# A new table of the order for a fused bucketed-attention and mixture-of-attention kernel

## The chip, the core and the metric

The kernel runs on one core of one Trainium2 chip. The metric is the time of one execution on the device, in microseconds (us). The core's engines are TensorE (matrix products; its loads of weights are shown apart), VectorE, ScalarE, GpSimd and SyncE; SyncE issues nearly all DMAs. In the profile they are called PE, PEld, DVE, ACT, POOL and SP.

## What is computed

First stage, for 4 batches and 8 heads of 768 rows with 64 columns: each row of q and of k gets a bucket from the signs of six projections; a query sees only keys of its own bucket. Second stage: the result, as 4 x 768 rows of 512, goes through a mixture of four causal attention heads ("experts"), of which each row uses the best two.

```python
q_bits = einsum(q, proj) > 0 ; k_bits = einsum(k, proj) > 0
mask   = q_bucket[:, None] == k_bucket[None, :]
scores = where(mask, scale * q @ k.T, -1e9)
attn   = softmax(scores) @ v                      # x, 4 x 768 x 512
logits = x @ w_gate ; topk = the two largest of 4
for e in range(4):
    a   = softmax(causal(scale * (x @ wq[e]) @ (x @ wk[e]).T))
    ye  = a @ (x @ wv[e]) @ wo[e]
    out += weight of e in the row * ye
```

## The kernel before

A unit is one head of the first stage (`("L", b, h)`, 32 of them) or one expert of the second (`("M", b, e)`, 16). The sequence `seq` lists the 48 units; the experts of a batch are mixed into the heads of the next one. For each unit, four kinds of work follow one another, always for several units at once:

- `max_steps(u)`: products of the queries with the keys into PSUM tiles `mx` (two buffers), in chunks of up to 512 columns. VectorE takes the maximum of each chunk into `pm` (`pmw` for the first eight heads). A chunk may consist of two products, for two blocks of queries, into one tile. Where a chunk meets the diagonal of a causal expert, VectorE adds the mask and takes the maximum in one operation (`scrap<-mx,causal`), one for each of the two halves.
- `shift_steps(u)`: the row of maxima is formed by VectorE (`negh`), turned by TensorE into a tile `misc`, copied as `row` by ScalarE or VectorE, and sent by a DMA into rows of the operand `qa`. It is subtracted inside the next products.
- `s_unit(u)`: `qk(c)` makes the products again, now the other way round and with the shift in them, into tiles `st` (three buffers). For a causal expert VectorE adds `mask_t` to the diagonal blocks in `st`. ScalarE makes the exponential twice, as `p` (32 bit) and `ph` (16 bit); `lo(c)` takes their difference `pl`, on GpSimd; `av(c)` multiplies `ph` and `pl` with the halves `vh` and `vl` of V into a tile `o` (one buffer). `normalise` ends the unit.
- `background` work: `prep_wide` and `prep_pair` split q and k into halves and make the signs `Mw` or `M` of the buckets (products with `pbh` and `pbl` or `pbd` into `misc`, one VectorE operation, four DMAs); `prep_v` scales V, splits it and sums it over the rows (VectorE, `misc<-vf`); `xt_steps`, `vproj_steps` (`mvh`, `mvl`, `lg`), `gate_steps`, `proj_steps`, `out_steps` make up the second stage.

Nothing of that is issued when it is written. A `Recorder` keeps all 10,808 operations with the engines that each may run on. `schedule()` then reads a table, `ORDER`: text in base 85, compressed, four rows of one byte for each operation. The first two rows say which of the operations that are left comes next, the third which of its engines it gets, the fourth how many filler products (`o<-busy`, 128x128, without use) go ahead of it:

```python
raw = np.frombuffer(zlib.decompress(base64.b85decode(ORDER)), np.uint8).reshape(4, n).astype(int)
for take, alt, fill in zip((raw[0] + 256 * raw[1]).tolist(), raw[2].tolist(), raw[3].tolist()):
    order += [self.filler] * fill
    o = left.pop(take)
    order.append((o, o.alts[alt]))
```

`issue()` walks that list, gives each new tile the next buffer of its pool, and hands the operation to its engine. Each engine works its own list off strictly in order. The waits between engines follow from the tiles: a second product into a tile comes behind a reader of that tile that the list puts between them. Since all operations are issued from one line of a helper, line 185 stands in nearly every row, and rows are told apart by the tiles' names.

Of the kernel before, what the change touches and what calls it, by code (L numbers as in the profile page):

```python
# [210 lines left out]
WN = 1  # L211
# [9 lines left out]
    "*DY=4WKEQ$T)m#l>BSjQnF>B7ri$iR@(sAfu$i|k>vl^vyjCu!`u$OVD&?w0dsVdy6J$yyHW7~7<o&VW=;){!8ICE+K+x-p1RLQEyrDI`-uTZ2<!@#*4SovW*ch>xhll`T*p=!}6+C)U"
    "$!4=TUDw>Omia4DaxTV~P~_m#zQ`$YI3$^TJf6)idc>&T|F}Qoi@V+9<1TWW34}Iy9Uo46f+ralZ?);N_R>ky>(gle&=4<Za?=kJxnHx~Zeg{uSG82%)u_U($K#XTs%9DyOND9m1V0G*"
    "Z-3Y23tIn;)iasytel>Ask5{C%&ehK?bxw{eNWY^oZ2(f6FPe9t<F<JLnjWE4wg39Rcc&@7U<2NV2>-{CEXR9rz({JwCRlA-0|tMvvIg|Z>`ijG2wO}28vYq<jJAYBS(e`n{Hm}?UnMC"
    "3f<G9kSmo2VMT|BvxPMVF;sWCtWh;g!aj0JGLWRLcgu-?H#n#a{`D9g|BYCT8kXp4xDoCbfq{X6pnqX`dEtM)|Grr1QB`#s2J7kRQOj3=2Tju{TFQaf=PFlFaFo02^?LlyKB}Nmg-TDp"
    "(Z~ye%JM5CjF(EV&xx$p8`fM)6rRI;Pmi};Hhty=kq0-a54%rT+%Z>3uLq1^saWB}!%@s^{!u;BA_EK!Wi~<EQQAX+iw_LQW`BRb8-`F1Dlss7ugq2|e6F0!7mGy=Mwk`LrUz#1l3Wt2"
    "o2{Gn_9|-FaDt5kMU|K2TqGh0cF=^3q>a;wj|RiUVgsA_-+JSJMf>$a*5z^s1x+(!v6w4Y|F4ijavGQM{B=6*)-^3_Qa<X>;T|ow#x|75^7~HR0wapz4}aKmIii@|hK()1E;wbQCza16"
    ")Amx<x<oN)Wy)o7%_%a)Vzc=(1r~pDQk-y(gBho6hMb9b(%A$^XRmXEO2rG0d(WB33iWlzDKK|QQeDXMt8hkp5dMf0Y*uvs75EjLA=Pnutio3`nT%v|IIbg!-ni-U`(v?qD8H}(<Ma4o"
    "Mi$sPJnt`;0}<0VG11*U=F5{{5nr~&Xp5hY#-hWS2xOJ%>3*A{K-L0@YMb4=qZxg=XKKfZa>O*}=jYAOeQu0#udc3!rrL}oa^vG8V-Ak6@8}KELq30#)-*+}(>0g-#EIK)zr8X)f69<2"
    "XFSuG@s%k9XIA&bI%kZD8K3-T+r$}Qbh^#K=@kz(=?;m(V6!<mzu-8#c;?KR#_V0HI%f?G@UVz4x1+e({B5xFkb)5E?Q2}k><2S2X%5#XZo6%H`P8YwlP6CiqxN@3y}p1b!`O$>x4WiR"
    "R#teJ`~1$G+m{d|q1fW$Vr=0jvDM<(9$;=|a&|TzACB!<V`6Hd#qz>JJT|v5w|!zFJ~$KGh9?!@IUXB}#kR*{D>j3>FJ~`&oozERvphEP?WsL~zBIFo=I)N{+zH-Y|LM$MWwWu}yP28g"  # L230
    "<-^N1v#YyoF3vpq=%ZtgJhJrg+!x!RrF$M)<828OlUn@v$FIW?z4Algl~?xffBEH?Z@>L(@4R#S{@eE7hJ)?+m%sergHLbf-A%lZeBP&=KmMJ^pLzU&&wc5!ryWl{^&0!6;bzS6OBh!!"
    "7czp#^;Q2fM#AyDL(?CB{Eo+HO?|`_2!*t}&#HkyK>ey;(`c{vE?w6zTsU~=rAuc_20X^Nc=4kCsD1|>|4Jf}crKTV$IqWXOx%C}$v?f%CUf)=l{(h{!~>~uMe*PF#ol}zf*^MM`1wYR"
# [1203 lines left out]
```

## Time and profile before

| | |
|---|---|
| median of three runs | 618.59 us (615.69 to 618.74) |
| the profiled execution | 618.5 us |
| its span, first to last instruction | 616.7 us |
| TensorE busy | 586.7 us, 95% |
| VectorE busy | 551.2 us, 89% |
| ScalarE busy | 525.6 us, 85% |
| GpSimd busy | 476.7 us, 77% |

The busy time of an engine is the union of its records. The end of a product is modelled, and products that follow each other closely overlap, so a busy TensorE is not one at its peak. The chain that ended last is followed back from the last instruction, at each step to what released it. In the rows, "out<-in" are the tiles written and read, "x4" is a count, and what stands behind a bar or in brackets is the idle time of the engine just before, with what ended it.

### The profile page before, as it was taken

The numbers are of one execution on the slowest core, as the hardware profiler recorded it, in microseconds if no ns is written. First come the engines' busy times: TensorE is split into PE (matmuls) and PEld (weight loads), VectorE is DVE, ScalarE is ACT, GpSimd is POOL, SyncE is SP. The second block draws the span as 40 slices with busy tenths as digits, with TensorE's granted clock in tenths as the row PEclk, the third lists the DMA queues.
The fourth block names the chain that finished last, engine by engine and source line by source line (L and its number), as shares of the span: only waits on it lengthen the run. The fifth ranks groups of instructions, "written<-read, shape, count | busy, mean of one in ns | idle before, by whom it ended". The sixth has DMA issues, their size and how long they took to land.

```text
span 616.7 us, 19646 instructions
## 1 busy us (share of the span) xinstructions
PE 586.7 (95%) x7331; PEld 416.3 (68%) x7331; DVE 551.2 (89%) x1514; ACT 525.6 (85%) x1162; POOL 476.7 (77%) x536
## 2 busy tenths in 40 slices
PE   8999999989999999889999999999999999999996
PEld 4778777766776666657666666767666767767663
DVE  7999989989999999878988999999989989757975
ACT  8989989999899999876978999997798989943873
POOL 7998988998688988866866889887757879941660
PEclk9999989999999999989999999999999999999999
DMA  5775522333213323331243231432122211102122
GB/s 146 223 186 155 131 70 74 85 93 101 53 41 100 79 51 78 93 83 36 62 129 88 55 95 32 134 95 60 48 61 82 46 42 42 50 14 47 51 101 103
DMA packets 35863, 51.07 MB, mean 83 GB/s; under 512 B 7764, under 2 KB 25656, under 8 KB 35768
## 3 DMA queue, kind: packets, MB, share of 16 engines
q1 hardware_dynamic: 35608, 49.83, 30.0%
q8 instruction: 57, 0.93, 0.6%
q14 instruction: 38, 0.31, 0.2%
q10 hardware_dynamic: 160, 0.00, 0.0%
HBM read 20.98 MB, written 6.29 MB: 44 GB/s over the span
## 4 chain that ended last, share of the span: by engine, by line
PE 50%; DVE 35%; ACT 6%; issue 5%; DMA 2%; SPq 1%; POOL 0%; DVEq 0%; ACTq 0%; POOLq 0%
PE misc L185 17%; PE st L185 14%; PE o L185 11%; DVE pm L185 9%; PE mx L185 8%; DVE misc L185 5%; DVE qk L185 4%; DVE pmw L185 4%; ACT p L185 2%; DVE xt L185 2%; DVE xp L185 2%; ACT ph L185 2%; DVE scrap L185 2%; DVE st L185 1%; DVE rden L185 1%
## 5 line engine op out<-in xcount | busy, mean ns | idle before, releaser
L185 POOL TENSOR_TENSOR pl<-p,ph 128x512 f16<-128x512 f32 (+1 forms) x377 | 417.0, 1130 | 117.7 <-PE o L185 35.1
L185 ACT ACTIVATE ph<-st 128x512 f16<-128x512 f32 (+1 forms) x380 | 218.8, 603 | 20.0 <-PE st L185 8.9
L185 ACT ACTIVATE p<-st 128x512 f32<-128x512 f32 (+1 forms) x380 | 220.3, 605 | 11.5 <-PE st L185 6.3
L185 PE MATMUL st<-qk,qk 128*128 128x256 f16 (+13 forms) x928 | 223.1, 325 | 3.6 <-DVE st L185 2.2
L185 PEld LDWEIGHTS <-ph 128*128 128x128 f16 x2944 | 169.9, 98 | 45.4 <-issue 14.2
L185 DVE TENSOR_REDUCE pm<-mx 128x2 f32<-128x512 f32 (+1 forms) x248 | 162.1, 673 | 3.8 <-PE mx L185 2.7
L185 PEld LDWEIGHTS <-pl 128*128 128x128 f16 x1472 | 136.9, 97 | 18.9 <-issue 3.8
L185 PE MATMUL mx<-qk,qk 76*128 76x512 f16 (+2 forms) x464 | 135.8, 330 | 11.7 <-DVE pm L185 7.6
L185 PEld LDWEIGHTS <-qk 128*128 128x128 f16 (+4 forms) x1248 | 108.2, 98 | 54.2 <-issue 14.5
L185 PE MATMUL o<-vh,ph 128*128 128x66 f16 (+1 forms) x1136 | 141.7, 195 | 2.2 <-DVE yn L185 1.4
L185 PE MATMUL o<-vh,pl 128*128 128x66 f16 (+1 forms) x1136 | 142.1, 194 | 0.0
L185 PE MATMUL o<-vl,ph 128*128 128x64 f16 x1136 | 140.8, 193 | 0.0
L185 PE MATMUL misc<-xt,wqk_h 128*128 128x384 f16 x256 | 58.8, 326 | 0.0
L185 DVE CUSTOM_DVE_ANT_0 scrap<-mx,causal 128x512 bf16<-128x512 f32 (+2 forms) x96 | 44.4, 462 | 7.1 <-PE mx L185 5.6
L185 DVE TENSOR_REDUCE pmw<-mx 128x2 f32<-128x512 f32 x68 | 45.1, 681 | 3.7 <-PE mx L185 3.4
L185 PE MATMUL o<-mvh,ph 128*128 128x65 f16 x336 | 40.0, 194 | 1.4 <-DVE xp L185 1.1
L185 PE MATMUL o<-mvl,ph 128*128 128x64 f16 x336 | 40.0, 192 | 1.4 <-DVE yn L185 1.4
L185 PE MATMUL o<-mvh,pl 128*128 128x65 f16 x336 | 40.2, 193 | 0.0
L185 PEld LDWEIGHTS <-xt 128*128 128x128 f16 x324 | 29.8, 97 | 10.7 <-DVE mvl L185 1.1
L185 PE MATMUL misc<-wvg_h,xt 128*128 128x260 f16 x192 | 33.4, 274 | 0.4 <-DVE mvl L185 0.4
L185 DVE TENSOR_TENSOR st<-st,mask_t 128x128 f32<-128x128 f32 x96 | 27.5, 292 | 6.5 <-PE st L185 5.0
L185 PEld LDWEIGHTS <-wqk_h 128*128 128x128 f16 x256 | 23.4, 97 | 13.4 <-issue 0.9
(216 smaller groups left out, 963.1 us busy)
## 6 DMA issues: line engine op xcount, KB each, us to landing
qk<-qk SPq DMA_DIRECT2D x128, 96.0 KB
...
```

The source lines that it names most:

```text
L185: getattr(getattr(self.nc, e), m)(*[real(x) for x in args], **{k: real(x) for k, x in kw.items()})
```

## The change

The text of `ORDER` is replaced; nothing else is. Of its lines the first ones stand here:

```diff
@@ -214,77 +214,76 @@
 MEANB = 3
 
 ORDER = (
-    "c-rlpd30RYec$K3`}TSJyf@36eZ_2;1v3~72I~;}LVzG4f&}+n5=kx8Vp581OQIxeakW^oEh~~@Q?(UUQXJbl&SF<doVICC>zuafNt&Mi(KdE-($oK%o}T{U_IKY57Lu|<$r1%p^U=Z6"
...
+    "c-rlpX^<S}dEck+Yr1>-?zyMuzOS9#nZ1wMUF?BtcX2I_#V!EiAP62JVG%qeng>LXA|;WbNQzNxN)bVdkt{NyBwMys#Z(d}A6!<Yq)ME!V}D4+uEeGIgUg9h<>Yy1W-o}cND&YLa(-1k"
...
 )
```

Decoded, the two tables hold the same 10,808 operations. They differ in this:

- The order of every engine. In TensorE's queue of 7232 products 1133 keep their place.
- The engine of 101 operations that two may run: 18 fewer for VectorE (1418 to 1400), 16 more for ScalarE, two more for GpSimd.
- The number of filler products, 61 in the old table and 73 in the new one; 14 of them now stand first in TensorE's queue.
- No reader of a tile `mx` or `st` stands any longer between two products into that tile; in the old table this is so for 10 tiles `mx` and 3 tiles `st`.

The new table is said to come from a search that used the true time of VectorE's sums of V, and in which all products into a PSUM tile come ahead of its readers, and these keep one sequence.

## Rows read from the trace of the kernel before

**Rows 1.** The page: span, and busy us (share of span) xinstructions of each engine.

```profile
span 616.7 us, 19646 instructions
PE 586.7 (95%) x7331; PEld 416.3 (68%) x7331; DVE 551.2 (89%) x1514; ACT 525.6 (85%) x1162; POOL 476.7 (77%) x536
```

**Rows 2.** The page: the chain that ended last, by engine.

```profile
PE 50%; DVE 35%; ACT 6%; issue 5%; DMA 2%; SPq 1%; POOL 0%; DVEq 0%; ACTq 0%; POOLq 0%
```

**Rows 3.** TensorE's waits: who waited for whom, us in total, times, longest.

```profile
PE mx L185 <- DVE pm L185: 7.6, 15, 2.3
...
PE st L185 <- DVE st L185: 2.2, 3, 1.2
```

**Rows 4.** Timeline of TensorE: start, us, product, [idle before]; first, second, last of nine parted products.

```profile
266.20 0.27 PE L185 MATMUL mx<-qk,qk 65*128 65x256 f16 x1 [2.25 <-DVE pm L185]
...
330.30 0.27 PE L185 MATMUL st<-qk,qk 67*128 67x128 f16 x2 [1.21 <-DVE st L185]
...
580.39 0.22 PE L185 MATMUL st<-qk,qk 128*128 128x128 f16 x1 [0.70 <-DVE st L185]
```

**Rows 5.** Timeline of VectorE ahead of 266.20: a sum of V and the parted tile's first reader.

```profile
262.79 1.56 DVE L185 TENSOR_REDUCE misc<-vf 128x128 f32<-128x768 f32 x1
...
265.73 0.41 DVE L185 CUSTOM_DVE_ANT_0 scrap<-mx,causal 128x256 bf16<-128x256 f32 x1
```

**Rows 6.** Windows: length, busy us of PE, PEld, DVE, ACT, POOL, clock; one wait.

```profile
264.00:266.20 2.20, 0.00 (x0) 0.00 (x0) 2.15 (x7) 1.90 (x6) 1.75 (x3) 1.00 0.07 16
...
267.30:270.70 3.40, 3.40 (x31) 1.43 (x28) 0.85 (x2) 1.41 (x3) 1.16 (x1) 0.50 0.39 125
...
74.89 0.47 PE L185 MATMUL mx<-qk,qk 76*128 76x512 f32 x1 [1.35 <-DMA qk<-Mw]
...
76.10:82.90 6.80, 6.80 (x59) 5.36 (x56) 4.82 (x8) 4.69 (x10) 4.20 (x5) 0.50 0.58 143
```

**Rows 7.** Groups of instructions: xcount | busy us, mean ns | idle before; sums and maxima of V.

```profile
L185 DVE TENSOR_REDUCE misc<-vf 128x128 f32<-128x768 f32 x16 | 25.1, 1571 | 0.0
...
L185 DVE TENSOR_REDUCE mqk<-natv 128x1 bf16<-128x768 f32 x14 | 13.2, 943 | 0.0
```

**Rows 8.** Groups: forms that change engine most, on VectorE; one on ScalarE.

```profile
L185 DVE CAST qk<-mx 128x384 f16<-128x384 f32 x24 | 13.1, 548 | 0.2 <-ACT mx L185 0.2
...
L185 ACT ACTIVATE qk<-mx 128x384 f16<-128x384 f32 x24 | 12.5, 528 | 0.1
...
L185 DVE TENSOR_SCALAR xt<-misc,xs 128x384 f16<-128x384 f32 x15 | 9.1, 608 | 0.9 <-PE misc L185 0.9
...
L185 DVE TENSOR_SCALAR ot<-misc,xs 128x512 f32<-128x512 f32 x4 | 3.0, 750 | 1.0 <-PE misc L185 0.5 <-PE o L185 0.5
...
L185 DVE TENSOR_SCALAR lg<-misc,xs 128x4 f32<-128x4 f32 x12 | 2.6, 220 | 3.2 <-ACT mvh L185 3.0
```

**Rows 9.** Groups of TensorE: fillers, and products of signs at the start and later; its first product.

```profile
L185 PE MATMUL o<-busy 128*128 128x128 bf16 x61 | 5.6, 230 | 0.0
...
L185 PE MATMUL misc<-natk,pbd 128*32 128x384 f32 (+1 forms) x22 | 4.1, 383 | 0.0
...
L185 PE MATMUL st<-natk,pbe 128*32 128x384 f32 x4 | 2.8, 847 | 0.0
...
2.55 0.41 PE L185 MATMUL misc<-one,pat 1*32 1x1 bf16 x4 [2.55 <-POOL pat L185]
```

**Rows 10.** The chain in order of time: start, us, what.

```profile
129.92 1.11 PE o L185 x37
...
159.19 1.95 PE misc L185 x12
...
266.65 0.34 PE st L185 x3
```

**Rows 11.** Timeline of one trip of a row of maxima: first and last product.

```profile
129.23 0.25 PE L185 MATMUL misc<-identh,negh 128*72 128x128 f16 x1 [0.45 <-DVE negh L185]
...
131.99 0.60 PE L185 MATMUL st<-qk,qk 78*128 78x512 f16 x2
```

More of the change, by code (lines that the diff above doesn't have):

```diff
@@ L221 @@
[L221 to L232, printed above, removed]
@@ L285 @@
[L285 to L287 removed]
+    "c-rlpX^<S}dEck+Yr1>-?zyMuzOS9#nZ1wMUF?BtcX2I_#V!EiAP62JVG%qeng>LXA|;WbNQzNxN)bVdkt{NyBwMys#Z(d}A6!<Yq)ME!V}D4+uEeGIgUg9h<>Yy1W-o}cND&YLa(-1k"
+    "Gnnaq`#qlH|GW(Vcez$rnU4iS%i)7q|B9dERhwnpmaL1q&gyQ(#d$o8B=S7X(QO!)OQlqb>R~vFvf`|Zx{nwqNS3a-2637p9ET)KB17tgo3OnVpW9VT6fiTFi)FP;lywZlX9SIa6PSr;"
@@ new lines @@
+    "VS@?#{i^EKY?m4^727aO)(`@MrZS2mk%nm=ltoQcce>^m7yU<$2p&NYIL9)^$EQt`Hw1n6n0JQKX6-(EV#=E2Eem};#@7ahhsVdqkLh~m@ITje{a}nIjjExl$F$w9^0Ip9Q0c)3CF+v<"
+    "H*vc_+wSZJbt|)lY-X%Y&Ydd!KbV)2(EzfBTTy!Q+;VDaC{fzLFbjo!Lti`bHDhscaKR9`mov+|gtYh7xT;zU3z}*OLf$>P!TkK_o)+QEt}UoLv%W!jW=7%aV?Iezt-+Czk=<L6<(-;5"
+    "FhK248dFoHy5o&_!{M-2txio%ag|E2%=T<ycsN%mo7HLw)^c_>AQ$|K(#+@cV{qh^9KdHggH8rhmSx2$N3=6PbsVQssn}eJGlN>h6Am}^x~|(X1Q*pDC#$G#Pcj%ZVu3&!$aqXgQC=$?"
+    "_M}p1Dz(gDbI|cz6i4NR{M9&fTv=IJ33Fn&81BG^+GIlUR4T<Mx8VyZvEDMeTRB`(9LHWU4jaalu``e~QZqASJB-sl$qWXq;Bl+n+=cMZQ3PU4NL&;H5xdoFEY?$x$Myd!X{_Qyw+@A<"
@@ new lines @@
+    "|KtgDP_$ewpW6#4#`3Z;Jgk0d$h1=Z{rxZWw_)BL8=BJU^+vtfY<eb+9zDQu%gaNTE{!N*u~Hcr2=(_jT1+<2c=*0z?*_xblf&ygxMvSLFITFy(|1|bQ+>U&=hu2y1*Yd@d)Ws6cCh`S"
+    "-htWKryI?gT8+zTBhB&3R))6IJD7PP8qEli@BS&QOJIEdj`{Iod2DogI+Om1KDoNar&7s3{$ouAM&k+QZ#jAZcy?fe-ig*=$Hu^UPMqii3hiDu=$_t&<Yk!MyFE-vD3{AKl2F_Z&*VLf"
+    "oMGg8eR=uCREkS--1Ao805q5=22!P3hld?^bqhUNt~|CC!v}^xB3Es%k83n6yRQ!{wx@@$?#vM7bYIDgr<zS#PoroRq1~}46VuU*vGUfracp(G$QL9jm(y7(t=g&@AKnDk-*E~q#|de{"
+    "v=&Tm8_5oU4opq?-Ob>H+npNaXt?BOKl>Ro6fYDCfjn0V)_$t%RbymCw*q>hz<>b-vJr5mqJf+uJ-LD1M7-N%wSYD{im}7^5dKb0?(x1Q2qC`&Gr&})r@t{hT>(Fq@}-jKd0EW8D5hS>"
@@ new lines @@
+    "NUn4~pQ~*m_VjR*Xwvp=kjO9ogPZ%wP)cYvg$aHJ7#E^_Bf|W=P>Vv~6sizB`4+-=M#OJRLv`uM5iI3i;|^vrPO1YeDOM`+iOhfD;pIIj3=XE#c$Uayyn>TU8h-ztNVFK~vC=-HgcXa4"
+    "aeID#9+t|R%h^WfqN;b`*fGnBknvzJ8qG!#U{%qUW0<vT_?=9KTY@OMK~^nIPA=;<?+;~078fm_rg7d=I~$3$`8B_4d%aV>#s)q0!8!`7yXUo?9S$7|%xiNk)Y(~bX6DB;2e)9_)B6Gn"
+    "%owFlADLJ^>|L3gVx$T2B492qhSZ6R!}raM1yyx;D^ne=PHg}w@)7XBY0~zR<5N=uWIJk1PMRctr_PUE!~XqaV@qRWjnUEL8?eT_N*+FZSXl;Ci1+)|T}w+#Ju_sqIUD^qFdF#r@DB8A"
+    "bar-jZZ;NM*dV%hIeO^Oo;^ESsU$i*y(2mkotukJ&&)K_(P*r>YuET81h+Z*)zyuU7cRu^xMS?-?T!;WbM?%b9fzjxyKiqSmfLl_e<-)-$dMy^4o}SQ-gV+%%h65C+xNtKz&!r=<8R=P"
@@ new lines @@
+    "E$&>p_-%0uU;Ck7eB!s)S(Dy=`|Z`W3+dzEI)DDnH`BMLU;ih-xwQD|`7eIvMIwoxlK$qY4sUMd(gROcpSk)R{w3YEuUw3li7Qu}mmNp5A`h4s!YPYOBvMB51=D=qFr!h+aZcZ9++iBr"
+    "6Ob`@^WJ;$Pm%XL`lzBwS~jce!)IG0Qz=IM%2)W<+S*zs^B{>|`htvo`tu2?FV26e#qF`tvAcTi6c;`h9r8XtvF8j39(?azg0RbgWPIk{dylj+4*UK7g9rUR`}g0wPEWu;vG2|e{1+a6"
+    "_yT#?(eopt=gy7ty^jE|e*aa($ncMU>*x5v4=(=Rd%^$iSHFMvgLe<{_fKDX5u5tf%hNA$zw_6V^WXZG*?jhyx87>LKKts-Z~y*wzA&@)rSGrvM}PGB?|ttZzt!ZXSAO`zS6=;tKUm>;"
+    "*OB#K*S-yW<x3a=wte*Jrw_h?aJ~Ne>(5@@|A)ihc=uhfrYkQYn|cI}=iqqjt+!mRXP^4QxpTkq#vAzSXRltp`qXQ$-FF{a@ps;N2ggstsz3Tqzk`$bo&Vyc$6iD{^5w689US6$^10`("
@@ new lines @@
+    "lCQlsKmWkR`$@!QI9_UVp>^iam+=>R!AOYbYtIq&`faz}OF#Yen>2k7bSc=8sjt3TC6-SU<SPVm=+M7>@hm}HI305xI(F>Xp(uWM1;_Dyd-fbUa1#GJyu}yM3)X~}rSX~b=iz+}Yx7?*"
+    "Y-X%R!jfVHK`cRMT<}i(ugvNyQKsoRIz~@U#yhvA52D|QU{J&Jd1L0>xiSul#lUGCSEJFRF+3(ol1xZ=+ZS|4jJTzpQCtaxalgk?=Y74hx2H$OUwP#fzJb5wZo%NZgxIx9`doZ|J`UNT"
+    "#RPNd&wQ-SayE+TjbUEn@mh^25vM48yqa8mmTIxQ%(9P%*be=0K;RwFdRe=VVm9y~a9NHNqEY^5S&nwoC}#*E&V<Hwonly4f@@`#&1U(Gu*wQTE+=e2^P51Kz%cLyHKglqd4OUmp^vf<"
+    "EX{(V;Ax(U3i35{R55E)Ly1H})6!nAm!d1y|6xE|n|_+e`Ka|AL_=oX(FQckB&kfaiNQ5$bch@bS-en`3P`#54CsDIEN-fs0S!X3p5yyExXb09nBb9lvM`K1^NXQaG)+GJ^wVsDOpuo^"
@@ new lines @@
+    "FGQbsB1#gZ_cx1rIBew}%B|zL@N_t}$vC1g77ma6PdudSf2H?FAR*cQzEE2N25U7Ru?3h@!X_=Z1p>Y5W|>fk2*Pyv{HE75A#PEBL4=3o(12w<X!%=Y;TS+4WM2od_n?>b{JDotDak?$"
+    "3g^U3#+^=kQgt~QmPnxzl}W)D%7<EZ=k@Y7Kw6f@sk&lnm~E?CP4)Zr_D%dOw2R@k6cttaALvj>)2>{(f(tS)J{}CZ1-Bb&HC7jduPd#^R}|$=sMsW-WtXDhhVNE*hWGi}2B9yZSEr3?"
+    "Djt54Z_2U;c5PityOt^x#lp{_iDHILdpvHp^e3W^<1lEH(=eaUZHXddF^pSRI1vd59_c_yX3AxlQn$dd9^TeC(^S<+2PVgQGIj>6x&Stl&3c?P!>UO};TbtHI!ca!MaE(*i+W5G;c#iA"
+    "rl8;Mlr8-msCHYU7cmaK<$JiQw=8m8Z*QT#4RAe{if8Cpo=L8cimKdo*Il{67H1*NwLd+M?axptmZkJ;{DEpb9&b&{J@-&FeP@ikqYMR>?SL0JsZj@1@=r%bqRx<ih-hCuXl>Z~Ud(YK"
@@ new lines @@
+    "xg2iH;QByIqu?z$iuuxC#I{2Hch;aNSopja2G5Jxj^7{fM>YutM>>Q+{QN~v54CR~SP7N;D5~ZQ5#C(3Q$^tz2z%P&F(cK*MTm-fa%=&N%l|#@yWb_e2-&hIAJ6H$_cc6#_x7Uj17B;%"
+    "EK4O@RK6q{jIMtkf`#smYMO#d6)3uie#P{_Ie%&2>$bjD78PS1hIhm7m$4NtIV}g4-8}7Pc<5;;#O*TrIgab&z)CsJwmAh{%fzAOS5WghI0WnWY~r}xAvU-LDX;}WPy^nOq6mi1vOFxQ"
+    "GHjfax7IOL4wW4;-`N#F@->XPIm>dJjKhHC(MhJPs4gGnp(s{N`U990C~rdI1c_?%d@u-$oXav9LW{WxRFv-Z+U+fXXiMIW5hMj&YTag>gnDI|8FCNii{ya=Hq9#r5`@WWnr!bYys&Hk"
+    "u3cP94vTRR!sCz|BK&0f#EHRl1`I5o%|aeylgZB{ler`t-m)bTkGo<-?7ZW3awifKiNx4gYh$6!?c}*Oas14gGi9sMI7!+ze%!l~Z6)vo*=Bf{OS<E3eAYD+>6@OOW~QcCz6wDb$EkBD"
@@ new lines @@
+    "@-wF>t?!_<s!*B!#l}Kz;GpLK;wQK5-roVb+^GmaEbaR2It!l(Km72+6uuZe)xK8{KYG;k-Jc-FFODCL$M@~WmM+}=;Mx`%c>Muf#XpTVe*;lpxeqaaFE!V9cz;Wup_@%FEWsU5ojS$C"
+    "AI_blPVB_y&m4E1Adej*PM&-SB>39evDMFh_Tt6pD$1gQFb1LTHQ}D2yM>`4fjEEio|ABKgI^a2^a+$!=@oi$7{Wv2)Aw_9J1^gr-vPhgo}tfX#?zovGH_aZBP3B1_AUrQr2@*TToU%9"
+    "fV&VBb~ceY#ye&i9P1Z^!J*Z<FyN}9tWfk7D+doQ@r!)E$h*u<aBvpCi&I+|ThUW`2Sx*8zNn8?{h_d~s~&mOKdTwT)|6+%Eo9X!GezXh9>%f?mX#Ax`zc9A4W!c%$cM!GZjMNUjS4(Y"
+    ">05SZ2Del7g+uic)##;av<wC|LRGRbGqrjuSKWRl$e8~AOr;f4OMQKdMOST4tz4*=T)n+Stw#2c<J%!(sWed<ER|dhoQlWNrBWPnK8`1dY|CY{NVVaKL^hk)q3c1t*#W-xI?6`6mLm~j"
@@ new lines @@
+    "x{UM)BmC$`D3gLxIiHxA2nI!a1Y@#-3p&=Com!0!1Sne9?V_K`W_`Xi#X&3z+8D-oUxH8s<L8y2qA{w0qTVxUPIs-Z1WzaUIIk#-$Hj9hG>%AfpuyDtplOZ}(f<cr%?Fu4V2Sl~WPps6"
+    "2E+WvRsyUgaa{<<;{`qxilLSMa?_<KmZeO<o#F1jLCRNqBfz?p+BYPb6v>uUOeU#hPl*)8qYw!qbT$%!3`;I7><t8VbAJCKwJ_>$S?kEiM8C<h178L7p;vkb*$pcD_K{5f3Y+tITrFJ}"
+    "|BNh8q7Ok>t<icT*gv>M^=Vq>thNasT3T|2f}zm=4jl}Kq2G%$NLZN7Mx%3q(k83Oop>GH4Baj>5O4(y(hzl1Bq6dxC=f}S(aMu$W`gC%Jlu#tire{{&O1djpaq#ZigLlS>4Hxn+k3+O"
+    ">zl(J`6-xk(xMWHW_)5R(l|s^6dP$_kO8&x!}=e>cqw{(d^kq^D~9Q8&Q-3l`gy=#=`TM|_0mkO!qY0pfrtNln%__jX&0YJ3Mi{U4d!%Y!~DEJ#-R2GD~+~0us8u#3ex+L(Vs#%g~FVo"
@@ new lines @@
+    "$VTfXBnW{(BvP-N=2$K_;tP_7L2e;Re#LRb&Fwh0Vg<QBBN*T7uajX$Z;RXDx-%<gXG_Z@CTx3*f}4eFR%kF3DwjF0>h=DZtB!G5w+AdcnRRng)R6k)dTZ-Amf;G!#4>dM>5M2zGf)q{"
+    "BgSK*KSsBufj7EN0HhZLl)#ruLDS49VN&$ZM<M^h;yCJKVVAlO?Z$QN!M1ym8$p`2K<CLa;b})WNr@}UL^LYNVLarOByf^BNeYET$q<@4>Ae=n>`;986~S)FT19cTBgsJ#7jcf`O}^u;"
+    "vd(dY=n*i{z}=cgOA^iez7&#zb92n%q8iz|m-Vr%7cwjz;~1L7DJ4L!_&33+bjs_^r$D7BDTVWRNRnmSMhO|EH~0(KtY?rEwS)Bw#X+IBm*jJ#{W&sS1TDd`B+KlpR+(pk?*M7cA;{!6"
+    "zxmBrJe?+pF?w{g+1vbQk%^6c_c+}{z~mDID8770`4M55RtSE9z{cWO!S+w<vD|TrMR>_N;YxT@%cM3Qj?e_P0r7V*K!Jc37&ZhVlkurxz2#w7;J`Cnx&uymabyr=YwFvfoNDi!nc*-A"
@@ new lines @@
+    "b)FZbhGa=UR((4#Pcmr}c^WD?AtFcOM5(0I6ovAE2JB=lH!pev9LPe8c=*jX-~8*K9b}=9VKuOH4XwT;Wj8C4Nc)YsEQ!J3ql{!4s^=lMD9d&mQ7I7lUa>7AH738Ns-hx_!Ncz6lkS)("
+    "I^M-$H+Vdh@CF?1E?^jn*L<2k+G<0W+F4nWP%AL|a{RsE`KVX)SP+f<zF^R&dwJ2#LpaZ5cu7$<H%_%y-2)En5u8$q_eA)d6zs`VdmwDht|O?ZZbpSK@1}TsmQA(Px8BD>HIz)UdZ~1<"
+    "6mo0%Hir(KJ9H?|x^u+R(hhzBLpqdBA_Xe4k;rVMx`Y0c=}KjCU~;ko1y?WR3$);zg&valrSkkH+`)r&&^sXh#&K#r$2Joa8+)G^%OsN!kLF@zbO~S<EA4$vX0kmInL@cRHhFG<gs?h("
+    "=N4v>QPM+Xq`7ZksZtpNaj>$<o@3PI%dnOkGAs)RAy^cJHuccPufQ_rIdD6Wuzjab*DAv!?1omP>4BxCm-qQsR+eZ*q3QiJy|nbmR?eTNq0mX<flpITZf&hFIYZs~;A2$Ad;a|Si*TI3"
@@ new lines @@
+    "|NQyGMDP+hcp7;0w13;x<DVsC!w)q`QU|FHDRlNguV)9m?}cND#o+Rjqw}4<K&`lIb&g$K-MO}Q@-}Av*y`L7{8K3LG6(OtcoB)id-j1_pFMku=jV5xd+OZXtN8KN<BvTC(dFs-sa52F"
+    "F!%#-EbRNYG)<u!oulSA-E)O<yQyVC82EGHAj(7pxd_+d?6R-K`g}OVG<%`#0Z-Z+`28$|nZcf(ignB|j+pO(!7!v1&}q#(OxsYdtCD2A2a+BESD-;NieAO0J>lu;u*VZ@&bebT%{?_`"
+    "_?s%-50RPP8n<~G!hYT~<L!I3qRFslXfNkZrRWe8gG{v(!66Su20DRlU?9@pAF0$Uc$4Y45KB=NTml0g12-CGD@C@z=Bw<|Ql%4Y+4ZVF!xcB5?zNxf?g0&zWB6QdN3}YY$u{}k-dqZj"
+    "HN&{FbcUwWPPAN3Q1SKJKaLy>N}NazvbAl4noLBfcDALr5Yj|3w!<!K|4l0vwE|7#aw_#B^fZG-`*QI~f$=f#o<bu+5@VQAEsa5$h3M=NZL3eKN<}S~Gq7m+yvjh;_mn1k4Y>8ROAb@a"
@@ new lines @@
+    "Z0;YsJMQY@`j9&HA72pc#x6B>0}B!CMkeu(y}Iv~FTY?Ou#a?lv5(h`;varoH_MEWTa_#MK2HCjVF|nGg!20isMvK`DEuS4_#<xpgIPXyeH`ZFmjI|6HZJ@owUCeR5?}Lt2D|R##jnHc"
+    "V7JzS<Da~ca4U;&>=rPon_HHAtnHor6)qq@#N}Nx?9yH3E?t}J(xvMTU8m~OjpW_2bVI_gJT~k`wvT-zON8C@i-3Lj&SPDd=}tg*hCi;uz`C}0!^VBf|H}-lYXF~+K4YKwE_V6YEC=>0"
+    "o{imd7Ke51=#$vR_iL!wulm(Zy+QEF$Pw7B(w`e{QQgGf<<@k!uH|-lpLT$`y8BaI-@El!7yIA~fOS{#W*ahgBOAbOSbwpP(A;mCrNX+N^9k-K_VJrs?1uOIMzzt^DBVQ<>+m`3dfnpJ"
+    "?o8YNufyxLvH!kR#QVLWbnO=({9o*B{ZEC6_iAd}KVo6fi@f<~`j_AE19XY+hN&)Hx^(H%rAwDCUAlDX(xpq6E?v5G>C&Z3mo8npbm`KiOP4NPx^(H%rOPLl{|}<*9S#"
```

74 lines of the change are left out of this document (16 added, 58 removed).

## The prediction

> **What bounds the kernel now.** I read the page first. The span is 616.7 us in an execution of 618.5 us, so 1.8 us lie outside it. TensorE is busy 586.7 us, VectorE 551.2, ScalarE 525.6, GpSimd 476.7 [rows 1]. The chain that ended last is half TensorE and 35% VectorE; ScalarE has 6% [rows 2]. So the reader should see two engines that take turns at being last, and 30.0 us (616.7 - 586.7) in which TensorE does nothing. That is the most that a new order could gain on TensorE, short of what the clock gives back. No product is added to or taken from the computation.
>
> Next the waits of TensorE. The largest is a product into `mx` that waits for VectorE's `pm`: 7.6 us in 15 waits. A product into `st` that waits for VectorE's `st` costs 2.2 us in 3 [rows 3]. The timeline shows which products these are. In the old table two products that write one PSUM tile are often parted: between them stands VectorE's reader of the first half. I decoded both tables (order, engine and number of filler products of each of the 10,808 operations) and counted tiles of `mx` and `st` whose first reader stands ahead of a later product into the same tile: 13 in the old table (10 of `mx`, 3 of `st`), none in the new one. In the trace the second product starts as soon as the first reader is done: at 266.20 where the reader ends at 266.14 [rows 4, 5]. Nine of the 13 show TensorE idle, for 2.25 + 1.21 + 0.38 + 0.36 + 0.36 + 0.19 + 0.55 + 0.28 + 0.70 = 6.28 us in the order of time [rows 4]; the other four show no wait. The three in `st` are all of the 2.2 us of `st` waits; the six in `mx` are 4.1 of the 7.6 us of `mx` waits.
>
> The longest of them shows how it comes about. On VectorE the first reader stands behind a sum of V (1.56 us from 262.79) and four operations more that follow it without a gap; it starts at 265.73 [rows 5]. TensorE does nothing from 264.0 to 266.2, and from 267.3 to 270.7 its granted clock is 0.50, the lower level, while VectorE is busy 0.85 of 3.4 us. A second such place: TensorE waits 1.35 us for the DMA `qk<-Mw`, and from 76.1 to 82.9 the granted clock is again 0.50 [rows 6].
>
> **The change part by part.** Only the table changes. All 7232 products stay; in TensorE's queue half of them move by at most 3 places and nine in ten lie between 13 places earlier and 14 later. It is the old plan revised, so I cost what differs in kind.
>
> *Products kept together.* Removed: the 6.28 us of idle time, and the low clock that follows the longest wait. In those 3.4 us TensorE was busy throughout at half speed, so 1.7 us are lost. Together 8.0 us. Not all of it reaches the end: where TensorE no longer waits for this reader, the next thing due from VectorE may be late. On the chain TensorE has 50 parts to VectorE's 35, so I let 50/85 = 0.59 through: **-4.7 us**, bounds 0 (VectorE is late everywhere) and -8.0.
>
> *The true time of the sums of V.* A sum takes 1571 ns, sixteen of them 25.1 us. A maximum over the same 128x768 input takes 943 ns [rows 7]. The diff doesn't say what the old search believed; if it priced the sum like that maximum, its plan was late by 628 ns sixteen times, 10.0 us of VectorE. The new table cannot shorten a sum, only place other work over it. At VectorE's share of the chain 10.0 x 0.35 = 3.5 us; I take half, **-1.8 us**. Bounds 0 and -3.5.
>
> *Engines.* The table gives VectorE 18 operations fewer, ScalarE 16 more, GpSimd two more (two `pl` subtractions of the last unit). The net moves from VectorE to ScalarE are nine `lg`, six `qk` halves, three `xt`, two outputs and two `mean`, less three `yth`, two `row` and one of the first halves. At the rows' means (220, 548, 608, 750 ns) [rows 8] this is 9 x 0.22 + 6 x 0.55 + 3 x 0.61 + 2 x 0.75 = 8.6 us, about 8 with the small ones and the two `pl` set off. ScalarE gains about as much, say 7: a `qk` half takes it 528 ns [rows 8]. VectorE's 8 x 0.35 = 2.8 us less ScalarE's 7 x 0.06 = 0.4 us gives **-2.4 us**, bounds 0 and -8. What hides it on ScalarE is its 91 us of idle time; where ScalarE is the last, the whole 7 us would show.
>
> *Fillers.* Sixty-one filler products become 73. Fourteen now stand at the head of TensorE's queue, where the first product of any kind began at 2.55 us [rows 9], so they fill a wait for GpSimd. If all twelve more lay on the path they would cost 12 x 0.092 (61 took 5.6 us) = 1.1 us. They could also gain: the four `st` records of the signs at the start took 847 ns where the same shape took 383 on the mean of the run [rows 9]. That is 4 x 0.46 = 1.9 us, and twice that with the like ones of `mx`; the records overlap in pairs, so 1.9 us in all. I take **0**, with -1.9 to +1.1 as the bounds.
>
> *Trips through a DMA.* Here the new table is tighter. I counted the TensorE work that stands between the transposing product of a row of maxima and the first product that reads that row. A product into `o` counts 30 ns (37 took 1.11 us on the chain) and one of 384 columns 162 ns (12 took 1.95 us) [rows 10]. The tenth percentile of this cover falls from 3.2 to 2.4 us and the median from 4.1 to 3.7. Of the 46 trips 2 had less than 2.7 us in the old table, 12 have so in the new one. What a trip needs: the product starts at 129.23, and its row is read at 131.99, after a copy and a DMA, with no wait shown: 2.76 us from start to start, 2.7 from the end of the product's slot [rows 11]. The new shortfall against 2.6 to 2.8 us is 3.3 to 5.7 us over all trips, the old one 0.8 to 1.2. The work between also takes longer than its bare count because TensorE waits elsewhere, so much of this is covered. The signs `M` go the same way: twelve trips whose least cover falls from 3.7 to 3.5 us and the median from 4.6 to 4.2. Priced as the rows are, this may add 2 us of shortfall. Bounds 0 and +6.5; I take **+2.9 us**, under half. Other loads go earlier: those of `natq` and `natk` in the first batch stand at least 11.9 us of products ahead of their use instead of 6.5, which hides them anyway.
>
> Sum: -4.7 - 1.8 - 2.4 + 0 + 2.9 = -6.0 us on 618.5: **612.5 us**. The profiled execution lies 0.1 us under the median of the three runs (618.59), so no step is needed between them.
>
> **The rivals.**
> - *The waits for `mx` stay.* The pool has two buffers, so a product waits for the reader of the product two back, and VectorE's queue is hardly shorter: at 264.3 to 265.7 it worked off that queue without a pause [rows 5]. Then of part one only the `st` waits go (2.2 x 0.59 = 1.3 us), parts two and three give half (2.1), and the trips take 2.9: 618.5 - 1.3 - 2.1 + 2.9 = **618 us**. For it: VectorE has 35% of the chain. Against: 4.1 of the 7.6 us of `mx` waits belong to products that write the tile they already hold [rows 4], and the parted product held up work that needs nothing of VectorE: three products into another tile, `st`, followed within 0.8 us of the one at 266.20 [rows 10]. Chance 0.25. (The Trainium skill, Perfetto Trace Analysis, Optimization Strategy, speaks for this rival: a gap that keeps returning on the engine that should be full can mean too few buffers for the next tile. For those 4.1 us the trace disagrees, for the other 3.5 it may agree.)
> - *The trips decide; slower.* One mechanism: products that read a row or the signs come before the DMA has landed. It decides if a trip needs 3.1 us, as most of the trips with little cover took, rather than the 2.7 of the shortest. Then 17 trips fall short, by 8.6 us against 1.6, and the signs add 2. [...] With the gains as forecast: 618.5 - 8.9 + 9.0 + 3.4 = **622 us**. Chance 0.13.
> - *More is set free.* The 1.35 us wait for `Mw` and the low clock behind it go too (cover 5.6 us against 5.2) and the parted products give all they cost: 612.5 - 3.3 - 1.35 - 2 = **606 us**. Chance 0.15.
> - *The table doesn't do what it says.* The sums of V stay where they were; only the parted products go: 618.5 - 4.7 + 2.9, about **617 us**. Chance 0.07, counted within half a per cent.
>
> **How the numbers follow.** The forecast has the other 0.40. A measurement of this kernel can tell about 0.5% (3.1 us), so faster means below 615.5 and slower above 621.7. Faster: 0.40 + 0.15 and a little of the first rival, 0.57. Same: 0.28. Slower: 0.15, which is the second rival and a little for what neither table's plan foresaw. The range takes in the forecast's own bounds, the fourth rival and the first, and reaches to the third: 605 to 620. The likeliest case alone spans 608 to 616.
>
> **What would show it right or wrong.** Right: no `PE st <- DVE st` wait, `mx <- pm` waits of some 3.5 us, no low clock near 267 us, TensorE's idle time near 25 us, VectorE's busy time near 543 and ScalarE's near 533. The trips are as I say if TensorE's waits and weight loads name DMAs of `row` and `M` for under 3 us in all. Wrong: TensorE's idle time at 30 us or more with other names in its waits; a new stretch of clock 0.50; or DMA waits of 6 us and more.

## The result and the profile after

The changed kernel takes **593.11 us** (median; 591.06 to 593.92), the kernel before on the same chip 618.66: a ratio of 0.9588 with a 95% interval of 0.9554 to 0.9623, 25.5 us less. The forecast was 612.5 us and its range ended at 605. The sign was right and the size was four times too small. The profiled execution took 593.65 us. In the runs beside the experiments the kernel before took 613.6 to 614.7 us where its mean granted clock was 0.999 or more, and up to 622.8 us where it was lower, while the changed kernel showed 0.999 or more in all its runs: so some 4 of the 25.5 us are stretches at the lower clock.

The page of the changed kernel: span, busy us (share) of each engine, and the chain that ended last by engine.

```profile
span 591.9 us, 19679 instructions
...
PE 576.6 (97%) x7343; PEld 414.6 (70%) x7343; DVE 542.7 (92%) x1496; ACT 523.5 (88%) x1178; POOL 477.7 (81%) x538
...
PE 71%; ACT 14%; DVE 6%; DMA 3%; issue 2%; POOL 2%; SPq 0%; ACTq 0%; POOLq 0%; DVEq 0%
```

Beside [rows 1] the span is 24.8 us shorter. TensorE's idle time fell from 30.0 us to 15.3 (591.9 - 576.6), its busy time by 10.1. VectorE had 35% of the chain [rows 2] and now has 6%.

TensorE's waits in the changed kernel: who waited for whom, us in total, times, longest.

```profile
PE st L185 <- DMA qk<-roww: 1.7, 1, 1.7
PE st L185 <- ACT ph L185: 1.1, 3, 0.6
PE mx L185 <- DVE pm L185: 1.1, 3, 0.6
PE o L185 <- DVE busy L185: 1.1, 1, 1.1
PE mx L185 <- DMA qk<-M: 0.9, 1, 0.9
PE st L185 <- ACT p L185: 0.8, 2, 0.6
PE st L185 <- DMA qk<-row: 0.6, 2, 0.4
PE misc L185 <- DVE yn L185: 0.5, 1, 0.5
PE mx L185 <- DVE pmw L185: 0.5, 1, 0.5
```

The wait for `pm` fell from 7.6 us to 1.1, and the wait of `st` for VectorE is gone [rows 3]. Others for VectorE, which the prediction had not priced, are gone or nearly so. In the kernel before they were these, in the same view:

```profile
PE o L185 <- DVE yn L185: 2.8, 2, 1.4
...
PE o L185 <- DVE xp L185: 1.7, 4, 0.9
PE mx L185 <- DVE pmw L185: 1.5, 4, 0.5
```

All rows of that view with VectorE as the releaser add up to 18.4 us in 35 waits before and 4.2 us in 10 after. Nothing comparable took their place: waits for ScalarE went from 1.1 to 2.1 us, for DMAs from 1.9 to 3.2.

The stretch 250 to 275 us, where the longest parted product stood: length, busy us of PE, PEld, DVE, ACT, POOL, granted clock, DMA share and GB/s; first before, then after.

```profile
250.00:275.00 25.00, 21.17 (x279) 15.10 (x278) 19.98 (x56) 19.75 (x44) 17.32 (x18) 0.93 0.28 79
```

```profile
250.00:275.00 25.00, 25.00 (x302) 18.19 (x301) 24.28 (x65) 21.04 (x50) 19.78 (x19) 1.00 0.38 103
```

After, TensorE never pauses here and the clock is never 0.50; nor is it near 76 us. Both low stretches of before [rows 6] are gone. They were 6.8 and 3.4 us of busy TensorE at half speed, which is 5.1 us lost in that execution.

So the 24.8 us of the span are 14.7 us of idle time (the waits for VectorE alone fell by 14.2), 5.1 us of clock, and 5.0 us of other busy time, whose cause stays open.

### The profile page after: what moved, and what is told of

Read it like the earlier page. It is cut to its first block, busy times and chain, and to the rows that moved or that the text cites. A ratio compares the mean times of both kernels' runs of the same rounds, so it can differ in the third digit from the quotient of the medians.

```text
span 591.9 us, 19679 instructions
## 1 busy us (share of the span) xinstructions
PE 576.6 (97%) x7343; PEld 414.6 (70%) x7343; DVE 542.7 (92%) x1496; ACT 523.5 (88%) x1178; POOL 477.7 (81%) x538
## 4 chain that ended last, share of the span: by engine, by line
PE 71%; ACT 14%; DVE 6%; DMA 3%; issue 2%; POOL 2%; SPq 0%; ACTq 0%; POOLq 0%; DVEq 0%
PE misc L185 23%; PE st L185 21%; PE o L185 16%; PE mx L185 11%; ACT p L185 5%; ACT ph L185 5%; DVE pm L185 2%; DVE misc L185 1%; ACT xt L185 1%; POOL pl L185 1%; ACT mx L185 1%; DVE pmw L185 1%; DMA qk<-M 1%; DMA qk<-roww 1%; ACT qk L185 1%
## 5 line engine op out<-in xcount | busy, mean ns | idle before, releaser
L185 POOL TENSOR_TENSOR pl<-p,ph 128x512 f16<-128x512 f32 (+2 forms) x379 | 418.4, 1129 | 86.2 <-ACT ph L185 19.7
L185 ACT ACTIVATE p<-st 128x512 f32<-128x512 f32 (+1 forms) x380 | 230.3, 646 | 11.3 <-PE st L185 9.8
L185 ACT ACTIVATE ph<-st 128x512 f16<-128x512 f32 (+1 forms) x380 | 228.2, 644 | 9.2 <-DVE st L185 2.1
L185 PE MATMUL st<-qk,qk 128*128 128x512 f16 (+13 forms) x928 | 224.4, 325 | 4.5 <-DMA qk<-roww 1.7
L185 PE MATMUL o<-vh,pl 128*128 128x66 f16 (+1 forms) x1136 | 139.3, 193 | 0.1
L185 PEld LDWEIGHTS <-qk 128*128 128x128 f16 (+4 forms) x1248 | 106.8, 98 | 46.3 <-issue 9.9
L185 PE MATMUL o<-vl,ph 128*128 128x64 f16 x1136 | 138.6, 192 | 0.0
L185 PE MATMUL mx<-qk,qk 76*128 76x512 f16 (+2 forms) x464 | 133.2, 326 | 2.9 <-DVE pm L185 1.1
L185 PE MATMUL misc<-xt,wqk_h 128*128 128x384 f16 x256 | 56.9, 325 | 0.0
L185 POOL TENSOR_TENSOR vl<-vf,vh 128x384 f16<-128x384 f32 x32 | 29.7, 930 | 9.9 <-ACT vh L185 9.8
```

The lines of the kernel that those rows point to most:

```text
L185: getattr(getattr(self.nc, e), m)(*[real(x) for x in args], **{k: real(x) for k, x in kw.items()})
```

## The experiments

Each kernel is the changed kernel's program with another list in `ORDER` (or one line changed, where shown). "The old list" is that of the kernel before. Ratios are to runs of the kernel before on the same chip; the gains in experiments 1, 3 and 4 are read from them. Waits are sums over the rows of TensorE's waits in the profiled execution.

**1. The old list with the 13 parted tiles kept together** (`old_joined`). The second product goes ahead of the first reader:

```diff
 product 1 -> mx
-reader 1 of mx
 (what stood between)
-product 2 -> mx
+product 2 -> mx
+reader 1 of mx
```

> The old table, and in it the later products into the 13 parted tiles stand directly ahead of the tile's first reader; nothing else moves. If the parted products are the cause (6.3 us of waits and 1.7 us of low clock behind the longest), about 610.5 us and no low clock near 267 us. If VectorE's next reader is simply late in their place, 616 to 619 us. If most of the 25 us comes from the order as a whole, this gives no more than 8 of them.

611.73 us, ratio 0.9914 (0.9869 to 0.996): 5.3 us gained. TensorE's waits:

```profile
PE mx L185 <- DVE pm L185: 3.9, 9, 0.9
PE o L185 <- DVE yn L185: 2.7, 2, 1.4
PE misc L185 <- POOL pat L185: 2.6, 1, 2.6
PE o L185 <- DVE xp L185: 2.0, 4, 0.9
PE mx L185 <- DVE pmw L185: 1.2, 4, 0.5
```

The `mx` waits fall by 3.7 us, the `st` waits for VectorE go, and so does the low clock at 267 us (1.00 from 265 to 272 us). Runs of both kernels with a mean granted clock of 0.999 or more differ by as much on the mean: 613.95 us before, 608.7 us here. The term of -4.7 us was of the right size. The waits for `yn`, `xp` and `pmw` stay.

**2. The same 13 tiles parted in the new list** (`new_parted13`), experiment 1 backwards.

> The new table with the same 13 tiles parted again: in 10 tiles mx the second product comes behind the first reader, in 3 tiles st the first reader comes ahead of the second product. If parted products cost what their waits showed, 599 to 601 us, with TensorE waits for pm and st that are absent in the new kernel. If TensorE finds other work or the wait is hidden, 593 to 595 us.

598.63 us, 0.9717 (0.9643 to 0.9792): 5.5 us more than the changed kernel's 593.11 (7.9 by the two ratios), with `mx <- pm` at 5.1 us in 10 waits. The price is no smaller in the better plan.

**3. The old list with quick sums of V** (`old_fastsum`). The sum reads neighbouring numbers, so means of V come from other numbers; its time is that of the maximum [rows 7].

```diff
-nc.vector.tensor_reduce(total, whole.rearrange("p j c -> p c j"), axis=AX.X, op=OP.add)
+nc.vector.tensor_reduce(total, vf.rearrange("p j c -> p (j c)")[:, 0:NT * 2 * D].rearrange("p (c j) -> p c j", j=NT), axis=AX.X, op=OP.add)
```

> The old table; the sums of V are taken over neighbouring elements, so that one should last near the 943 ns of a maximum over 768 elements instead of 1571 ns. This changes what is summed: the means of V, used only for rows without a partner, are other numbers. If the old plan was wrong by the length of the sums and this is the cause of most of the gain, about 600 to 605 us. If at VectorE's share of the chain, 615 us. If the sums hardly mattered, 617 to 619 us.

608.54 us, 0.9885 (0.9802 to 0.9968): 7.1 us gained. The group of the sums (xcount | busy us, mean ns | idle before) and the first of TensorE's waits:

```profile
L185 DVE TENSOR_REDUCE misc<-vf 128x128 f32<-128x768 f32 x16 | 15.2, 951 | 0.0
```

```profile
PE mx L185 <- DVE pm L185: 5.7, 10, 2.3
...
PE st L185 <- DVE st L185: 2.2, 3, 1.2
```

Taking 9.9 us from VectorE (25.1 to 15.2) gave 7.1: 0.7 us for each, though the interval (2.0 to 12.2 us) is wide.

**4. Both in the old list** (`old_joined_fastsum`).

> The old table with the 13 tiles joined and with the shorter sums of V (other numbers for the means). Alone the two gave 5.3 and 7.1 us. If they are separate causes, 12.4 us under the kernel before: a ratio of 0.980. If they are one cause (a VectorE that is late, seen at two places), 7 to 8 us: 0.988. What is then left up to the new kernel's 0.959 is neither of them.

604.3 us, 0.9784 (0.9723 to 0.9846): 13.3 us. The two gains add up (5.3 + 7.1 = 12.4). Of the 25.5 us, half is explained by them; some 12 us are not. TensorE's waits for VectorE are still 10.8 us in 21.

**5. The new list with quick sums** (`new_fastsum`) and **with sums twice as long** (`new_longsum`, each number added twice and the mean halved). The first is the edit of experiment 3.

```diff
-nc.vector.tensor_reduce(total, whole.rearrange("p j c -> p c j"), axis=AX.X, op=OP.add)
+nc.vector.tensor_reduce(total, whole.rearrange("p j c -> p c j")[:, :, None, :].to_broadcast([128, 2 * D, 2, NT]), axis=AX.XY, op=OP.add)
```

> The new table with the same shorter sums (other numbers for the means of V). If the new plan has hidden the sums' true time, 592 to 594 us, as without it. If VectorE's time simply counts everywhere, 10 us of it less at the new chain's 6% give 0.6 us, and at the old chain's 35% 3.5 us: 589.6 us.

> The new table, each sum of V taken twice over (and the means scaled by half), so that it lasts about 1.5 us more than the plan has for it, 24 us of VectorE in all. If what hurts is time that the plan does not know of, at the rate of the old table's 7.1 us for 10, then 17 us more than the new kernel: 610 us. If VectorE's time has a price that does not depend on the plan, at the 1.8 us for 10 that shorter sums gave the new table, 4.3 us more: 597 us.

Quick sums: 591.33 us, 0.9596 (0.9523 to 0.9668), no difference from the changed kernel. Long sums: 614.38 us, 0.9954 (0.9924 to 0.9983), 21 us more. Some 3 of the 21 are a stretch at a lower clock (0.52 from 36.7 to 43.5 us of its profile; the mean clock of its ten runs is 0.985 to 0.998). In the long one:

```profile
L185 DVE TENSOR_REDUCE misc<-vf 128x128 f32<-128x1536 f32 x16 | 47.6, 2973 | 0.0
```

```profile
PE mx L185 <- DVE pm L185: 6.5, 9, 1.4
PE misc L185 <- DVE qk L185: 2.6, 3, 1.2
PE mx L185 <- DVE pmw L185: 2.6, 4, 1.0
PE mx L185 <- DVE xt L185: 1.4, 1, 1.4
```

The same operations, at the same places: 9.9 us less gain at most 1.8 us, 22.5 us more cost 21, or some 18 without the clock. The new list has room for the sum as long as it is, and not for one nearly twice as long, though VectorE idles for 49 us of the span. Where in between the room ends was not measured.

**6. Order and engines crossed** (`old_newengines`, `new_oldengines`): the old order with the new choice of engine, and the other way round. Decoded operation by operation, the two tables give 82 operations another engine; the 101 named above and in what was expected is too many, while the net moves (18, 16 and two) hold.

> The old order with the new table's choice of engine for the 101 operations that differ. If VectorE's 8 us less work count by themselves, as the prediction had it, 2.4 us faster: 0.996. If they carry the rest of the gain, 8 us and more: 0.987. If the choice only fits the order it was made with, the same time or slower.

> The new order with the old choice of engines, so VectorE has 18 operations more. If VectorE's time counts by itself, 2.4 us over the new kernel: 595.5 us. If the choice carries the rest of the gain, 600 to 603 us. If it makes no difference in this order, 593 us.

| | old engines | new engines |
|---|---|---|
| old order | 1 | 1.0195 (1.0134 to 1.0256) |
| new order | 1.0062 (1.0025 to 1.0099) | 0.9588 (0.9554 to 0.9623) |

Waits of the old order with new engines, then of the new order with old engines:

```profile
PE mx L185 <- DVE pm L185: 8.5, 15, 2.3
PE st L185 <- ACT p L185: 3.1, 6, 1.4
PE o L185 <- DVE yn L185: 2.7, 3, 1.4
```

```profile
PE st L185 <- POOL pbe L185: 2.7, 1, 2.7
PE st L185 <- ACT p L185: 2.4, 6, 0.7
PE mx L185 <- DVE pm L185: 2.4, 6, 0.6
PE o L185 <- DVE none L185: 2.3, 3, 1.7
```

Either half alone is slower than before, by 12.7 and 4.2 us; together they gain 25. The first has VectorE busy 6 us less than before (545.1) and is slower all the same. What an engine choice is worth can't be read from busy times.

**7. Only 28 short operations on their old engines** (`new_smallold`): 14 `row` copies and 14 `none`, of 150 to 275 ns each.

> The changed kernel with its own order, but the old choice of engine for 28 short operations alone (14 that write the rows, 14 that zero or copy, 150 to 275 ns each, some 6 us of busy time in all that change engine). The whole old choice cost 28 us in this order. If an operation on another engine costs by its length: 592 to 593. If it costs by where it now stands in that engine's queue, ahead of or behind work it was not placed by: 596 or more.

600.23 us, 0.9713 (0.9655 to 0.9771): some 7.5 us more than the changed kernel, while VectorE's busy time rises by 1.0 us and ScalarE's by 1.3. The largest wait is now this one:

```profile
PE o L185 <- DVE none L185: 2.3, 3, 1.7
```

`none` takes 0.2 us, and TensorE waits up to 1.7 us for it: in VectorE's queue a sum of V, a `row` and two `qk` run ahead of it without a pause, from 112.31 to 115.01 us. An operation on another engine costs by its place there, not by its length. These waits are 2.3 of the 7.5 us; the rest lies in smaller ones and was not traced one by one.

**8. Where along the list the other 12 us lie.** Four hybrids, all without parted tiles and with quick sums: one list up to a place, the other list from there, cut where `normalise` begins for unit 5 (the "norm"; some 100 us) or for unit 24 (some 325 us).

```diff
-order = old[:]
+order = new[:k] + [o for o in old if o not in new[:k]]     # and the same with old and new changed over
```

> The changed kernel's table up to the norm of the second stage (list position 1663, some 100 us), then the old table with the parted products kept together; the sums of V are the fast ones, so means of V come from other numbers. Both neighbours of this kernel are measured: the old table joined with fast sums 604.3, the new table with fast sums 591.3, so 13 us lie between. Theory A, the first 100 us carry about 5 us of it (the wait for Mw, the stretch at the low clock behind it): 599. Theory B, the gain of the order is spread over the whole list: 602. Theory C, nothing of the head counts, since the VectorE is caught up later: 604.

> The other half: the old table (joined, fast sums) up to the same norm (list position 1652), then the changed kernel's table. Theory A: 596 to 597. Theory B: 593. Theory C: 591. If both halves lose more than they should together (sum of the two losses over 13 us), the plan is worth something only as a whole.

> The changed kernel's table up to the norm of unit 24 (list position 6042, some 325 us), then the old table with the parted products kept together; fast sums, so means of V come from other numbers. Between the two whole tables with fast sums lie 604.3 and 591.3 us. TensorE's waits for VectorE after 320 us are 4.3 us in the old joined one and 0 in the new one, between 104 and 320 us 5.2 and 1.9. Theory A, the gain lies all along the list in these waits and nothing is caught up: 597 to 598, TensorE's waits for VectorE some 8 us. Theory B, what the first half gains the second half gives back: 602 to 604. Theory C, only the middle part (100 to 320 us) counts: 592 to 594.

> The other half: the old table (joined, fast sums) up to the norm of unit 24 (list position 6030), then the changed kernel's table. Theory A: 596 to 597, TensorE's waits for VectorE some 6 us. Theory B: 591 to 593. Theory C: 601 to 603.

| which part is the new list | us | ratio | TensorE's waits for VectorE |
|---|---|---|---|
| none (experiment 4) | 604.3 | 0.9784 (0.9723 to 0.9846) | 10.8 us in 21 |
| up to unit 5 | 605.9 | 0.9791 (0.9726 to 0.9855) | 12.1 in 22 |
| up to unit 24 | 598.55 | 0.9679 (0.9616 to 0.9742) | 8.0 in 17 |
| from unit 24 | 599.79 | 0.9689 (0.9625 to 0.9753) | 7.3 in 16 |
| from unit 5 | 592.41 | 0.9597 (0.9537 to 0.9656) | 2.9 in 10 |
| all (experiment 5) | 591.33 | 0.9596 (0.9523 to 0.9668) | 3.8 in 10 |

The first 100 us give nothing that can be measured (at a mean granted clock of 0.999 or more it is 603.3 us in one run against 602.4 in two of experiment 4). After that each half gives about half: 5.8 and 4.5 us of 13.0 by the medians, 6.5 and 5.9 of 11.6 by the ratios. Nothing that one half gains is lost again in the other. With the old list from unit 24 on, the old list's own waits are back. From 325 us on:

```profile
PE o L185 <- DVE yn L185: 1.2, 1, 1.2
PE mx L185 <- DVE pm L185: 1.2, 2, 0.9
PE o L185 <- DVE xp L185: 0.9, 2, 0.7
PE misc L185 <- DVE mvl L185: 0.9, 2, 0.4
```

In the changed kernel no wait of TensorE for VectorE is listed after 320 us. Between the profiles of experiments 4 and 5 TensorE's waits for VectorE fall by 7.0 us and those for DMAs from 3.6 to 0.2, and 10.2 us at the lower clock (5.1 us lost) are gone. So the greater part of the rest is some ten waits for VectorE, each between 0.2 and 1.5 us, at many places. The hybrids show where along the list it lies; how it divides between these waits, the DMAs and the clock was not tested one by one.

**9. One wait mended by hand** (`old_joined_fastsum_mw`): experiment 4, with one VectorE operation that makes `Mw` and its first two DMAs put directly behind the last product that they need.

```diff
 product -> misc
+misc -> Mw (VectorE), Mw -> qk, Mw -> qk (DMAs)
 (other work)
-misc -> Mw (VectorE), Mw -> qk, Mw -> qk (DMAs)
```

> The old table with the 13 tiles joined, with the shorter sums of V (other numbers for the means), and with one operation of signs Mw and its first two DMAs moved up: the operation stands right behind its products and ahead of the sum of V, the DMAs ahead of a load of natq and two copies on SyncE's queue. If the wait for these DMAs and the low clock behind it (1.9 us and 10.2 us at half speed in the run without the move) are the next cause, 597 to 599 us. If TensorE waits as long for something else there, 604 us. The new kernel's 593 would then leave 4 to 6 us for all the rest.

605.61 us, 0.9818 (0.9774 to 0.9862): no gain. The wait for `Mw` falls from 1.9 us in experiment 4 to 0.5; this one follows 2.7 us later, and the clock is 0.50 from 75.6 us all the same:

```profile
PE misc L185 <- DVE xt L185: 2.2, 2, 1.8
```

```profile
75.60:82.40 6.80, 6.80 (x62) 5.35 (x62) 4.80 (x9) 4.45 (x9) 3.60 (x4) 0.50 0.52 138
```

VectorE works its queue off in order, so what goes earlier in it can make something else late.

**10. The new list without the 14 fillers at its head** (`new_nohead`), and **the changed kernel again** on that chip (`new_again`).

```diff
-fill[:first_product] = 14
+fill[:first_product] = 0
```

> The new table without the 14 filler products that stand at the head of TensorE's queue. If they only fill a wait, as the prediction had it, the same time as the new kernel, within 1 us. If they bring the clock up earlier, 1 to 2 us slower. If they hold the first products up, up to 1 us faster.

> The changed kernel once more, beside the others on their chip: 590 to 594 us.

592.63 us, 0.96 (0.9557 to 0.9644), and 591.72 us, 0.9588 (0.9545 to 0.9631): no difference. The fillers stand where TensorE waits for GpSimd in any case.

**11. A try for a faster kernel: V stored so that the true sum reads neighbours** (`new_cj`).

```diff
-VF = [con.tile([128, NT, 132], FT, name=f"vf{i}") for i in range(NV)]
+VF = [con.tile([128, 132, NT], FT, name=f"vf{i}").rearrange("p c j -> p j c") for i in range(NV)]
```

> The new table, with the scaled V kept in SBUF with its six blocks innermost, so that the sum reads neighbours and is right; ScalarE then writes, and ScalarE, GpSimd and a few products read, with a stride. If only the sum changes, 1.8 us faster than the new kernel, as with the shorter sums. If the strided side costs what the sum gains, the same or slower: 593 to 597 us.

603.66 us, 0.9788 (0.9754 to 0.9822): 12 us slower than the changed kernel. The groups that touch V, and the first of TensorE's waits:

```profile
L185 POOL TENSOR_TENSOR vl<-vf,vh 128x384 f16<-128x384 f32 x32 | 36.1, 1130 | 13.3 <-ACT vh L185 13.3
...
L185 ACT ACTIVATE vh<-vf 128x384 f16<-128x384 f32 x32 | 31.7, 993 | 0.1
L185 ACT ACTIVATE vf<-natv,cs 128x384 f32<-128x384 f32 x32 | 31.4, 1033 | 0.0
...
L185 DVE TENSOR_REDUCE misc<-vf 128x128 f32<-128x768 f32 x16 | 15.2, 948 | 2.1 <-ACT vf L185 2.0
```

```profile
PE st L185 <- ACT ph L185: 4.3, 10, 0.8
PE st L185 <- ACT p L185: 1.9, 5, 0.6
```

The sum is 0.62 us shorter, but ScalarE's `vf` takes 1033 ns for 651 and `vh` 993 for 590. ScalarE now has 27% of the chain. As the new list hides the long sum anyway, there was nothing to win. No kernel that computes the same was faster than the changed one.

## Why the prediction was wrong

*Products kept together, -4.7 us:* right in size, in part by luck. 5.3 us by experiment 1, 5.5 to 7.9 by experiment 2; the signs named for it (no wait of `st` for VectorE, no low clock near 267 us) are there. But 0.59 of 8.0 us is not how it came about. In experiment 1 the `mx` and `st` waits fell by 5.9 us and nearly all of that came through, and since the 5.3 us show between runs without the lower clock too, its 1.7 us are not among them. The share of the chain was no better a price here than for the sums.

*The true time of the sums, -1.8 us with bounds 0 and -3.5:* **this step failed.** Experiments 3 and 4 give 7 to 8 us, outside the bounds. I priced VectorE's time at its share of the chain, 0.35, and halved it. The chain follows one path; it doesn't tell what an us of an engine is worth. Measured, an us of VectorE that the list left no room for costs 0.7 to 0.95 us (experiments 3 and 5; the upper figure holds some 0.15 of clock), and one that it has room for 0.2 at most. The change moved the sums from the first kind to the second. (Whether the old search really took the sum to be as quick as the maximum no run can show.) The true time was in the rows from the start: 1571 ns against 943 [rows 7]. (The Trainium skill, SBUF — State Buffer, Door 1: The DMA port swizzle, says that reads which leave a 16-byte line each time lose speed; the trace agrees, with 1571 ns against 951 in experiment 3.)

*Engines, -2.4 us:* **wrong in kind.** Busy times came out partly as forecast (VectorE 542.7 against 543, ScalarE 523.5 against 533), but the choice by itself costs 12.7 us in the old order and its absence 28 in the new one. It has no price of its own, so a term for it doesn't belong in the sum.

*Fillers, 0:* right (experiment 10). A reading in it was wrong: the 383 ns are a mean over products of 384 columns and others of one column, and those of 384 alone took 498. The four `st` records still take 844 ns in the changed kernel, so nothing was gained there.

*Trips through a DMA, +2.9 us:* too high. Waits for DMAs rose by 1.3 us to 3.2, hardly over the 3 us that I named (in the profile of `new_again` they are 2.0); the longest is the 1.7 us for `roww`. The rival in which they decide did not happen. The 3.4 us in its sum, for a lower clock behind a wait of over 1.3 us on a trip, no run shows: in the changed kernel the clock stays 1.00 behind those 1.7 us, as it does in the kernel before behind its wait of 1.4 us at 605 us. In one kernel of experiment 8 it fell behind 0.91 us on a trip, for 10.2 us.

*What had no term:* **the larger failure.** I listed TensorE's waits for VectorE only so far as I could name the cause in the two tables (6.28 us and the sums). The view held 18.4 us of them. The new list did away with most: some 12 us beyond the parted tiles and the sums, all along the list after the first 100 us (experiment 8), for which the sum had nothing. Finding that nine in ten of TensorE's products move by less than 15 places, I called the new table the old plan revised and priced only differences in kind. But waits of 1 us hang on a few places in one queue: 13 moves took 5.9 us of them away (experiment 1), and 28 short operations on other engines cost 7.5 us (experiment 7). The 30 us of idle time that I gave as the most a new order could gain was the better guide, and TensorE's idle time, forecast at 25 us, was 15.3.

*The rivals.* That the `mx` waits stay because the pool has two buffers is refuted: with two buffers they fell from 7.6 us to 3.9 by 13 moves alone, and to 1.1 in the new list. Whether a third buffer would have done the same in the old list no run shows. (The Trainium skill, Perfetto Trace Analysis, Optimization Strategy, says that returning gaps can mean too few buffers; here 6.5 of the 7.6 us went with the number of buffers unchanged.) The rival at 606 us came nearest. It was right that the low clock at 76 us would go, but experiments 8 and 9 show that this wait was not the key: the first 100 us of the new list bring nothing.

What stays open: why the search found the better places, by the truer time, by the rule on products and readers, or by running longer. The tables don't tell.
